# Attention and a squared-ReLU layer on one core: scores in two operations a tile, late loads apart, a new order of all work

## Chip, core and metric

The kernel runs on one core of a Trainium2 chip. Time is device microseconds of a whole execution. A core has five engines that work side by side and wait for each other by semaphores: PE (TensorE, matrix products), DVE (VectorE), ACT (ScalarE), POOL (GpSimd, which here mostly issues transfers) and SP (SyncE, which issues the others). Each runs its own instructions strictly in the order in which they were written.

## What is computed

```python
# q, k, v: 4 batches, 8 heads, 768 positions, 64 wide; local window 96, 8 global keys
scores = q @ k.T / sqrt(64) - slope[h] * dist          # kept where global or local
a = softmax(scores); attn = a @ v                       # -> x: 3072 tokens, 512 wide
h = x @ w_in                                            # 512 -> 2048
out = (max(h, 0) ** 2) @ w_out                          # 2048 -> 512, float32
```

## The kernel before

**Tiles.** The 3072 tokens are 24 tiles `j` of 128 (six to a batch), and two tiles are one block `blk` of the second layer, so there are 12 blocks. A tile needs the keys of itself and of the tile before it, but the first of a batch (0, 6, 12, 18) only its own; the eight global keys and values are copied into each tile's key and value buffers (`gk`, `gv`).

**A tile's steps**, with the names that the order list uses. `tr.0.j` and `tr.1.j` transpose q and k on PE (tiles 0 to 7; later tiles are transposed by a transfer, `T.j`, that SP issues), and `T.0.j`, `T.1.j` copy them out of PSUM. `sc.j` are the scores: 16 small matmuls (8 for the first tile of a batch) of contract dimension 64, line 599, into four PSUM banks (two). For tiles 0 to 2 `bias.j` first writes the mask and slope into those banks by matmuls (line 579). `exp.j.odd.g` is the exponential of one bank on ACT, `mul.j.g` multiplies two of them by the masks on DVE, `pv.j.hf` is the product with v for four heads (line 748), `norm.j.hf` the division on DVE. `trx.j` (PE, tiles 0 to 7) or a transfer `xT.j` transposes the result for the second layer.

**The second layer.** Blocks 0 and 1 use plain products `s1.blk.s` (line 1061) with `relu` and `sq` behind them, later blocks a seven-product scheme: `h.blk.g.p1` to `p7` (line 950) with copies `u` and additions `c` between them and squares `q`; then `s2` (lines 1212 and 1339) with the sums `sum`, copies `part` and results `o`, and the store `st`.

**Loads.** q and k of tile 0 come by SP in float32 (`plain`, line 319). All else comes through POOL's queue with a cast to bfloat16: `ld.k.1`, `ld.win.6.0`, `ld.v.0` and so on for the tiles up to 5 and the weights (line 307), and `load.j` for tiles 6 to 23, one operation that issues v, q and k of the tile one behind another (line 310):

```python
def emit_load(e, j=j):
    load_v(j)
    load_part(0, j)
    load_part(1, j)
```

**Order.** Nothing is scheduled at run time. The string `ORDER` lists all operations by name; the program emits them in that order, each on the engine named behind `@` (A is ACT, V is DVE, P is POOL; without it the first that the operation allows), with the PSUM banks named behind the colon. An engine's order is thus the order of its names in the list. Eight matmuls on zeros (line 372) run before the list, and eight more (`warm`, line 532) stand in it.

Of the kernel before, what the change touches and what calls it, by code (L numbers as in the profile page):

```python
# [62 lines left out]
T.1.4@V xT.1@V pv.2.1:0 ld.k.5 ld.win.2.0 exp.3.1.1 gk.3@A ld.win.2.1 norm.2.0 s1.0.3:2 mul.3.0 s1.0.6:4 ld.win.4.0
tr.0.4:7 ld.q.5 ld.v.4 norm.2.1 mul.3.1 relu.0.6@A s1.0.3#2 gv.2@P pv.3.0:3 norm.3.0 trx.2:5 T.0.4@A pv.3.1:6
ld.win.1.0 norm.3.1 ld.win.0.1 xT.2@A sc.4.0:1047 exp.4.1.1 exp.4.1.0 tr.1.5:3 T.1.5@A s1.0.2:5 trx.3:6 xT.3@V
ld.win.0.0 ld.win.5.0 s1.0.2#2 s1.0.2#3 s1.0.2#4 relu.0.3@V exp.4.0.1 ld.v.5 gv.3@P exp.4.0.0 gk.4@V sq.0.6@V
relu.0.2@A s1.1.3:7 ld.win.7.0 relu.1.3@A load.6 s1.1.6:0 mul.4.1 tr.0.5:6 mul.4.0 sq.0.3@V s1.1.2:3 T.0.5@A ld.wout.3
pv.4.0:2 ld.wout.1 sq.0.2@V sc.5.0:4157 ld.wout.0 s1.0.4:6 relu.1.2@A exp.5.1.1 s1.0.1:3 sq.1.3@A exp.5.0.0 relu.0.4@V
s1.1.4:7 ld.wout.2 norm.4.0 pv.4.1:4 gv.4@P norm.4.1 sq.0.4@A load.7 exp.5.1.0 sq.1.2@A relu.1.4@A s1.0.0:6 gate.9
ld.wout.4 mul.5.0 s1.0.0#2 sq.1.4@A s1.0.0#3 s1.1.5:2 trx.4:1 exp.5.0.1 relu.1.6@V s1.1.1:4 ld.wout.5 s1.0.1#2  # L70
relu.1.1@A E0.1 mul.5.1 relu.1.5@A pv.5.0:7 s1.1.7:0 s1.1.0:5 sq.1.1@V norm.5.0 ld.wout.6 E0.0 sq.1.5@V tr.1.6:4
sq.1.6@A pv.5.1:2 relu.1.7@A tr.0.6:7 s1.0.0#4 norm.5.1 xT.4@A sq.1.7@A h.2.0.p2:0 ld.wout.7 T.1.6@V h.2.1.p2:1
trx.5:2 xT.5@V relu.1.0@A sq.1.0@A gate.14 h.2.0.p1:5 xs.2.0 s1.0.5:4 sum.1.2 s1.0.7:2 relu.0.1@A xs.2.1 gate.10
sum.1.0 sum.1.1 relu.0.0@A T.0.6@A sc.6.0:36 wsum.0.0 sum.1.3 sq.0.0@A sq.0.1@A s2.0.0.0:7 relu.0.7@A s2.0.1.0 load.9
exp.6.0.0 xs.2.2 s2.0.2.0 exp.6.1.0 s2.0.3.0 s2.0.0.1:2 s2.0.1.1 wsum.2.0 relu.0.5@A sq.0.7@A s2.0.2.1 load.8 mul.6.0
wsum.1.0 s2.0.3.1 tr.0.7:3 tr.1.7:6 gate.15 isum.0.0 h.2.1.p1:4 T.0.7@A s2.0.4.0 isum.0.1 s2.1.p1.0:3 isum.3.1 T.1.7@A
sq.0.5@A pv.6.0:6 isum.1.1 s2.0.4.1 s2.0.5.1 u.2.0.1@A c.2.0.c11 s2.0.5.0 gate.11 u.2.1.1@A h.2.1.p6 q.2.0.c11@A
isum.1.0 T.8 s2.0.6.1 u.2.1.2@A s2.0.6.0 isum.3.0 pv.6.1:0 h.2.0.p6 wsum.2.1 wsum.0.1 s2.1.p1.1 s2.0.7.1 c.2.1.c11
norm.6.0 gate.13 o.0.1@V st.0.1 s2.0.7.0 h.2.1.p7 part.1.p1@A s2.1.p6.0 u.2.0.2@A o.0.0@A u.2.1.3@A h.2.0.p7 h.2.1.p4
T.9 norm.6.1 wsum.3.0 u.2.0.3@A sc.7.0:1762 c.2.1.c21@A wsum.1.1 h.2.1.p5:0 c.2.1.c22 q.2.1.c11@A s2.1.p2.0:4  # L80
exp.7.1.0 exp.7.0.0 isum.2.1 load.10 h.2.0.p4 exp.7.0.1 mul.7.0 exp.7.1.1 s2.1.p2.1 isum.2.0 s2.2.p1.0:7 q.2.1.c21@A
mul.7.1 h.2.0.p5:1 s2.1.p6.1 part.1.p6@A trx.6:6 gate.12 c.2.0.c21@A load.12 pv.7.0:2 xT.6@A c.2.0.c22 q.2.1.c22@A
q.2.0.c22@A s2.2.p1.1 h.2.1.p3 s2.1.p7.0 wsum.3.1 o.1.p2 norm.7.0 h.2.0.p3 pv.7.1:5 s2.1.p7.1 q.2.0.c21@A st.0.0
c.2.1.c12 s2.1.p5.0 s2.1.p5.1 part.1.p7@A q.2.1.c12@A s2.1.p4.0 T.10 s2.1.p4.1 c.2.0.c12 gk.7@V q.2.0.c12@A o.1.p5
o.1.p4@A sc.8.0:6201 st.1.1 part.2.p1@A s2.1.p3.0 norm.7.1 sum.2.0 sum.2.1 s2.1.p3.1 trx.7:5 xT.7@V o.1.p3 h.3.0.p1:3
exp.8.1.0 gk.8@V h.3.1.p1:2 exp.8.0.0 exp.8.1.1 exp.8.0.1 h.3.0.p2:6 xs.3.0 u.3.1.1@A sc.9.0:1540 s2.2.p6.0 mul.8.0
xs.3.1 mul.8.1 u.3.0.1@A h.3.0.p6 exp.9.0.1 exp.9.1.1 gv.7@V h.3.1.p2:4 c.3.0.c11 h.3.1.p6 c.3.1.c11 exp.9.0.0
pv.8.0:0 s2.2.p6.1 pv.8.1:6 load.11 norm.8.0 u.3.1.2@A s2.2.p2.0:1 sum.2.2 gv.8@P q.3.1.c11@A norm.8.1 xT.8 h.3.1.p7
h.3.0.p5:4 u.3.0.2@A h.3.0.p7 s2.2.p2.1 exp.9.1.0 st.1.0 part.2.p6@A xs.3.2 u.3.1.3@A q.3.0.c11@A h.3.1.p5:0 s2.2.p7.0
u.3.0.3@A mul.9.1 mul.9.0 s2.2.p7.1 c.3.1.c22 T.12 c.3.0.c22 pv.9.0:6 h.3.1.p3 o.2.p2 h.3.0.p4 c.3.1.c12 load.15  # L90
norm.9.0 q.3.1.c22@A h.3.0.p3 s2.3.p1.0:5 s2.3.p1.1 c.3.0.c12 q.3.0.c22@A pv.9.1:0 c.3.0.c21@A part.2.p7@A norm.9.1
q.3.1.c12@A h.3.1.p4 q.3.0.c12@A h.4.0.p1:3 c.3.1.c21@A s2.2.p5.0 part.3.p1@A gk.9@V sc.10.0:6402 s2.2.p5.1
q.3.0.c21@A sum.3.0 sum.3.1 s2.2.p4.0 s2.2.p4.1 exp.10.1.0 sum.2.3 exp.10.0.0 exp.10.0.1 h.4.0.p2:4 T.11 u.4.0.1@A
exp.10.1.1 gk.10@V gv.9@A s2.3.p6.0 o.2.p5 mul.10.0 c.4.0.c11 xT.9 h.4.1.p1:6 o.2.p4@A mul.10.1 s2.2.p3.0 s2.2.p3.1
q.3.1.c21@A s2.3.p2.0:0 sum.3.2 u.4.1.1@A pv.10.0:2 pv.10.1:4 s2.3.p6.1 xs.4.0 gate.17 o.2.p3 part.3.p6@A xs.4.1
s2.3.p2.1 norm.10.0 h.4.0.p6 h.4.1.p6 q.4.0.c11@A gv.10@A norm.10.1 u.4.0.2@A load.13 s2.3.p7.0 sc.11.0:7124 u.4.1.2@A
sum.3.3 h.4.0.p7 h.4.1.p7 xs.4.2 exp.11.1.0 o.3.p2 exp.11.0.0 u.4.0.3@V s2.3.p7.1 sc.12.0:17 exp.11.1.1 exp.11.0.1
gate.16 xT.10 h.4.0.p4 c.4.0.c21@A mul.11.0 st.2.0 mul.11.1 h.4.1.p2:4 c.4.1.c11 exp.12.1.0 s2.3.p5.0 pv.11.0:2
pv.11.1:3 s2.3.p5.1 norm.11.0 part.3.p7@A h.4.0.p5:7 q.4.1.c11@A u.4.1.3@A norm.11.1 h.4.1.p5:4 q.4.0.c21@A gate.20
s2.3.p4.0 c.4.0.c22 load.14 s2.3.p4.1 h.4.0.p3 T.13 gate.18 load.16 c.4.1.c22 exp.12.0.0 h.4.1.p4 q.4.1.c22@A h.4.1.p3  # L100
xT.11 s2.4.p2.0:2 h.5.0.p1:3 q.4.0.c22@A o.3.p5 mul.12.0 c.4.0.c12 o.3.p4@A c.4.1.c21@A u.5.0.1@A c.4.1.c12 T.15
s2.3.p3.0 q.4.0.c12@A s2.3.p3.1 q.4.1.c12@V q.4.1.c21@A h.5.0.p2:1 o.3.p3 sc.13.0:5764 st.3.1 st.2.1 h.5.1.p1:0
# [1329 lines left out]
```

## Time and profile before

| | |
|---|---|
| runs, us | 198.84, 198.79, 200.68; median 198.84 |
| span of the profiled execution, us | 197.6, so that 1.2 us of the median lie around it |
| PE / DVE / ACT / POOL busy, us | 191.9 / 173.2 / 163.0 / 80.4 |
| matmuls on PE | 2776 |
| chain that ended last, by engine | PE 95%, DVE 2% |

The span runs from the first to the last instruction. A group's row gives its busy time, the mean time of one instruction, and the idle time ahead of it with what ended that. The profile lists no own time for the profiled execution, so sums below are made on the span, and the 1.2 us are added.

### The profile page before, as it was taken

How to read it: one execution, taken by the hardware profiler on the slowest of the kernel's cores; microseconds unless marked ns; L12 is line 12 of the kernel's file. 1: busy time of each engine (PE TensorE's matmuls, PEld its weight loads, DVE VectorE, ACT ScalarE, POOL GpSimd, SP SyncE). 2: the span in 40 equal slices, each digit the busy share in tenths (PEclk: the TensorE clock that was granted, in tenths of full speed). 3: DMA queues.
4: the chain of work that ended last, by engine and by line, in shares of the span. 5: the costliest groups of instructions: out<-in, count | busy, mean ns of one | idle time of the engine just before them, and what ended most of it. 6: DMA issues, size and time to landing. Idle time of an engine off the chain costs nothing.

```text
span 197.6 us, 6777 instructions
## 1 busy us (share of the span) xinstructions
PE 191.9 (97%) x2776; PEld 169.6 (86%) x2776; DVE 173.2 (88%) x423; ACT 163.0 (82%) x335; POOL 80.4 (41%) x101
## 2 busy tenths in 40 slices
PE   7989999999999999999999999999999999999993
PEld 3578999866989999899989999989899989999992
DVE  8159869999999999799999999999899999989872
ACT  6379989966999898999789998998989879774750
POOL 8999988586045309603192903080410001000000
PEclk9999999999999999999999999999999999999999
DMA  6999999999999999999999999999695711114023
GB/s 127 153 158 171 181 181 185 182 202 159 139 209 191 75 200 88 145 174 210 151 129 203 114 124 194 160 121 92 136 81 116 154 55 56 27 30 163 0 106 106
DMA packets 111857, 26.91 MB, mean 136 GB/s; under 512 B 103379, under 2 KB 109011, under 8 KB 111827
## 3 DMA queue, kind: packets, MB, share of 16 engines
q0 software_dynamic: 80256, 13.37, 91.8%
q1 hardware_dynamic: 31570, 13.11, 32.5%
q8 instruction: 21, 0.34, 0.6%
q14 instruction: 10, 0.07, 0.1%
HBM read 27.26 MB, written 6.29 MB: 170 GB/s over the span
## 4 chain that ended last, share of the span: by engine, by line
PE 95%; DVE 2%; issue 1%; ACT 0%; DVEq 0%
PE bank L1212 35%; PE bank L950 32%; PE bank L1061 7%; PE bank L599 6%; PE bank L748 5%; PE bank L1339 4%; PE bank L372 2%; PE bank L506 2%; PE bank L532 1%; DVE qkT L433 1%; PE bank L816 1%; PE bank L579 0%; ACT qkT L429 0%; DVE o L1287 0%; DVE v L433 0%
## 5 line engine op out<-in xcount | busy, mean ns | idle before, releaser
L1015 ACT ACTIVATE hs<-hr 128x512 bf16<-128x512 f32 x72 | 44.8, 641 | 5.1 <-DVE hr L995 4.7
L665 ACT ACTIVATE esc<-bank 128x512 bf16<-128x512 f32 x78 | 42.9, 614 | 1.3 <-PE bank L599 1.0
L1212 PE MATMUL bank<-wsum,hsum 128*128 128x256 bf16 x264 | 36.2, 273 | 0.0
L1212 PEld LDWEIGHTS <-hsum 128*128 128x128 bf16 x360 | 32.1, 98 | 4.1 <-issue 0.5
L995 DVE CUSTOM_DVE_ANT_0 hr<-bank,early 128x512 f32<-128x512 f32 x45 | 30.4, 685 | 2.5 <-PE bank L950 1.5
L950 PEld LDWEIGHTS <-win 128*128 128x128 bf16 x480 | 29.7, 98 | 1.0
L950 PEld LDWEIGHTS <-qk_first 128*128 128x128 bf16 x480 | 29.7, 98 | 1.0
L429 ACT COPY early<-bank 128x512 f32<-128x512 f32 x42 | 24.5, 591 | 3.6 <-PE bank L950 3.3
L690 DVE TENSOR_TENSOR at<-esc,E 128x1024 bf16<-128x1024 bf16 x39 | 26.7, 696 | 0.1
L1212 PEld LDWEIGHTS <-hs 128*128 128x128 bf16 x264 | 24.0, 98 | 2.6
L310 POOL DMA_DIRECT2D qk<-in_q_dram x18 | 16.0, 890 | 21.9 <-DMA qkT<-qk 20.6
L1212 PE MATMUL bank<-wout,hs 128*128 128x256 bf16 x176 | 24.9, 273 | 0.0
L310 POOL DMA_DIRECT2D v<-in_v_dram x18 | 16.0, 888 | 18.3 <-DVE v L480 14.9
L950 PE MATMUL bank<-xT,win 128*128 128x128 bf16 x320 | 23.4, 219 | 0.0
L431 POOL COPY v<-v 8x520 bf16<-8x520 bf16 x8 | 5.7, 718 | 43.3 <-PE bank L748 43.3
L950 PE MATMUL bank<-xs,qk_first 128*128 128x128 bf16 x320 | 22.8, 219 | 0.0
L779 DVE TENSOR_TENSOR x<-bank,rs 128x256 bf16<-128x256 f32 x48 | 20.4, 425 | 1.7
L865 ACT ACTIVATE hr<-bank 128x512 f32<-128x512 f32 x33 | 19.4, 598 | 1.3 <-PE bank L950 0.4
L748 PE MATMUL bank<-v,at 128*128 128x65 bf16 x352 | 17.8, 193 | 0.0
L1287 DVE TENSOR_TENSOR o<-bank,part 128x256 f32<-128x256 f32 (+2 forms) x34 | 13.8, 410 | 3.3 <-PE bank L1212 3.2
L429 ACT COPY part<-bank 128x256 f32<-128x256 f32 x29 | 10.9, 375 | 7.1 <-PE bank L1212 6.9
L310 POOL DMA_DIRECT2D qk<-in_k_dram x18 | 16.1, 897 | 0.9 <-DMA win<-in_moe_w_in_dram 0.5
(92 smaller groups left out, 367.0 us busy)
## 6 DMA issues: line engine op xcount, KB each, us to landing
out_dram<-o SPq DMA_DIRECT2D x22, 256.0 KB, 2.5
v<-in_v_dram POOLq DMA_DIRECT2D x24, 128.0 KB, 5.6
qk<-in_q_dram POOLq DMA_DIRECT2D x18, 128.0 KB, 5.0
qk<-in_k_dram POOLq DMA_DIRECT2D x18, 128.0 KB, 5.8
wout<-in_moe_w_out_dram POOLq DMA_DIRECT2D x8, 256.0 KB, 8.5
win<-in_moe_w_in_dram POOLq DMA_DIRECT2D x6, 256.0 KB, 6.9
...
```

What stands on the lines that cost most here:

```text
L310: nc.gpsimd.dma_start(out=dst, in_=src)
L429: nc.scalar.copy(dst, src)
L665: nc.scalar.activation(out=tiles[tag, j, g][:, odd], in_=tiles.pop(("sc", j, odd, g)).rearrange("p a c -> p (a c)"), func=Act.Exp, scale=s ...
L690: nc.vector.tensor_mul(at, tiles.pop(("esc", j, g)), bias)
L748: nc.tensor.matmul(out=po[:, hi, :], lhsT=tiles["at", j, g][:, odd, at * P : (at + 1) * P], rhs=v_sb[kj][:, h, :], start=(i == 0), stop=(i ...
L779: nc.vector.tensor_tensor(out=x[:, 4 * hf : 4 * hf + 4, :], in0=po[:, :, :D], in1=rs.to_broadcast([P, 4, D]), op=Alu.mult,)
L865: nc.scalar.activation(dst, src, Act.Relu)
L950: nc.tensor.matmul(out=tiles["h", blk, g, bank][:, n], lhsT=left_[:, s, k], rhs=right_[:, k], start=opens and n == 0 and k == 0, stop=k == ...
L995: nc.vector._custom_dve(TENSOR_ADD_SAT, out=hr, in0=src, in1=tiles.pop(("u", blk, g, i)), s0=float("inf"), s1=0.0,)
L1015: nc.scalar.activation(hs, hr, Act.Square)
L1061: nc.tensor.matmul(out=hT[:, c, cols], lhsT=w_in_sb[s][:, kt, c * P : (c + 1) * P], rhs=tiles["xT", blk][:, kt, cols], start=(kt == 0), st ...
L1212: nc.tensor.matmul(out=tiles["acc", blk, bank][:, cols], lhsT=left_[:, s], rhs=right_[:, cols], start=first and s == 0, stop=s == NSTEP - ...
```

## The change

Four edits. (1) The scores of a tile that isn't the first of its batch become two operations, `sc.j.0` (heads 0 to 3) and `sc.j.1` (heads 4 to 7), each with two banks; so do the `bias` matmuls of tiles 1 and 2. The matmuls are the same. (2) `load.j` becomes `lv.j`, `lq.j` and `lk.j`, each with a wait of its own and a place of its own. (3) `warm` asks for its bank like other operations. (4) `ORDER` is another list throughout: other places, other banks, and for some copies another engine.

```diff
 ORDER = """
-tr.0.0:0 warm:7 tr.1.0:1 T.1.0@V bias.0.0:23 T.0.0@A sc.0.0 ld.win.3.0 exp.0.0.0 ld.k.1 tr.1.1:4 bias.1.0:5670 T.1.1@V ld.q.1
-tr.0.1:1 ld.v.0 exp.0.1.0 T.0.1@V sc.1.0 exp.1.0.1 pv.0.0:2 ld.q.2 tr.0.2:3 norm.0.0 ld.k.2 T.0.2@V ld.k.3 exp.1.1.1
-pv.0.1:4 tr.1.2:1 bias.2.0:7203 ld.v.1 norm.0.1 exp.1.1.0 ld.q.3 tr.1.3:6 gk.1@A T.1.2@A sc.2.0 exp.1.0.0 T.1.3@V
...
+ld.k.1 ld.win.6.0 ld.q.2 ld.q.1 tr.0.0:0 ld.win.2.1 ones.6 ld.k.2 tr.1.0:1 T.0.0@A ld.k.3 warm:2 T.1.0 E0.0 ld.v.0
+ld.v.1 bias.0.0:23 sc.0.0 ld.q.3 tr.0.2:4 exp.0.0.0 tr.0.1:5 T.0.2 tr.1.1:6 ld.win.2.0 bias.1.0:70 T.0.1 T.1.1@A
+bias.1.1:12 ld.v.2 exp.0.1.0 sc.1.1 sc.1.0 exp.1.0.1 ld.q.4 tr.1.2:4 gk.1 bias.2.0:56 exp.1.0.0 T.1.2 tr.1.3:3 exp.1.1.1
...
-    SETS = {}
+    SETS = {j: [(0,), (1,)] for j in range(NT) if j % TPB}
...
-            def emit_load(e, j=j):
-                load_v(j)
-                load_part(0, j)
-                load_part(1, j)
...
-            ld = plan.op(
-                ("load", j), {"POOLQ": 2.6}, emit_load,
-                deps=qk_users[slot(j)] + v_users[j % NV] + [ones.get(j), gate], key=base, ready=issue[0],
-            )
+            for name, f, users in (
+                ("lv", load_v, v_users[j % NV] + [ones.get(j), gate]),
+                ("lq", lambda j: load_part(0, j), qk_users[slot(j)]),
+                ("lk", lambda j: load_part(1, j), qk_users[slot(j)]),
+            ):
+                ld = plan.op(
+                    (name, j), {"POOLQ": 0.9}, lambda e, j=j, f=f: f(j), deps=users, key=base, ready=issue[0],
+                )
+                land[name[1], j] = plan.op(("data" + name, j), {"DMAQ": 2.7}, None, deps=[ld])
...
-            plan.op(("warm",), {"PE": 0.216 * NKEEP}, emit_warm, key=base)
+            wusers = []
+            wusers.append(plan.op(
+                ("warm",), {"PE": 0.216 * NKEEP}, emit_warm, key=base, takes=(*G, [wusers]),
+            ))
```

Three places show what the list moves. **PE at the start.** `plain` is q of tile 0 (into bank 0) and then k of tile 0 (into bank 1); DMAHW1 is the landing of that k. Before, the transposes of q were followed by the eight `warm` matmuls, of which the first row below is the last, and by these:

```order
L532 MATMUL bank_7_114<-early_103 128x512
L506 MATMUL bank_1_108<-ident32_100,plain_70 128x128 [waits DMAHW1_49]
L506 MATMUL bank_1_108<-ident32_100,plain_70 128x128 x3
L579 LDWEIGHTS early_103 [waits DVE_49]
L579 MATMUL bank_2_109<-pb0_105,early_103 128x128
```

and now, from the transposes of q to the first `warm`:

```order
L502 MATMUL bank_0_107<-ident32_100,plain_70 128x128 [waits DMAHW0_49,DVE_49]
L502 MATMUL bank_0_107<-ident32_100,plain_70 128x128 x3
L502 MATMUL bank_1_108<-ident32_100,plain_70 128x128 [waits DMAHW1_49]
L502 MATMUL bank_1_108<-ident32_100,plain_70 128x128 x3
L528 LDWEIGHTS early_103
L528 MATMUL bank_2_109<-early_103 128x512
```

The eight `warm` matmuls stood ahead of the transposes of k, and stand behind them now.

**POOL's queue at the start.** Before (`qk_first` holds q and k of tiles 1 to 5: k1, q1, then q2, k2 and k3, then q3, k4; v_71, v_72 and v_73 are v of tiles 0, 1 and 2):

```order
L307 DMA win<-in_moe_w_in_dram 128x4x256
L307 DMA qk_first<-in_k_dram 128x8x64
L307 DMA qk_first<-in_q_dram 128x8x64
L307 DMA v_71<-in_v_dram 128x8x64
L307 DMA qk_first<-in_q_dram 128x8x64
L307 DMA qk_first<-in_k_dram 128x8x64 x2
L307 DMA v_72<-in_v_dram 128x8x64
L307 DMA qk_first<-in_q_dram 128x8x64
L307 DMA qk_first<-in_k_dram 128x8x64
L307 DMA v_73<-in_v_dram 128x8x64
```

and now (k1; q2 and q1; k2 and k3; q3):

```order
L305 DMA qk_first<-in_k_dram 128x8x64
L305 DMA win<-in_moe_w_in_dram 128x4x256
L305 DMA qk_first<-in_q_dram 128x8x64 x2
L305 DMA win<-in_moe_w_in_dram 128x4x128
L305 DMA qk_first<-in_k_dram 128x8x64 x2
L305 DMA v_71<-in_v_dram 128x8x64
L305 DMA v_72<-in_v_dram 128x8x64
L305 DMA qk_first<-in_q_dram 128x8x64
L305 DMA win<-in_moe_w_in_dram 128x4x128
L305 DMA v_73<-in_v_dram 128x8x64
```

v of tile 2 was the eleventh transfer of the queue and is the twelfth, with two half pieces of w_in ahead of it beside a whole one.

**PE around tile 2's product with v.** Before, `pv.2.0` followed the scores of tile 3 and the transposes of tile 1's result:

```order
L816 MATMUL bank_7_114<-ident_99,x_319 128x128
L748 LDWEIGHTS at_315
L748 MATMUL bank_5_112<-v_2_73,at_315 128x65 [waits DMASW2_49]
L748 LDWEIGHTS at_315
L748 MATMUL bank_5_112<-v_1_72,at_315 128x65 [waits DVE_49]
```

Now it follows the transposes of q of tile 3 (`qk_first`), and the scores of tile 3 stand behind it:

```order
L502 MATMUL bank_6_113<-ident_99,qk_first_66 128x128
L747 LDWEIGHTS at_305 [waits Activation_49]
L747 MATMUL bank_4_111<-v_2_73,at_305 128x65 [waits DMASW3_49]
L747 LDWEIGHTS at_305
L747 MATMUL bank_4_111<-v_1_72,at_305 128x65 [waits DVE_49]
```

The wait on DMASW is that for v of tile 2. Behind it on PE are now `sc.3.0` and `sc.3.1`, side by side. On PE the two halves of a tile stand side by side in all of the 20 split tiles but tile 2, and twice the scores of two tiles stand together (7 and 6, 18 and 17), so PE comes to scores 23 times where it came 24 times.

More of the change, by code (lines that the diff above doesn't have):

```diff
@@ L63 @@
[L63 to L102, printed above, removed]
@@ new lines @@
+T.1.4 lk.6 s1.0.2#3 relu.0.6 norm.3.0 pv.3.1:0 sc.4.1:71 sq.0.6 sc.4.0:24 ld.win.1.0 norm.3.1 s1.0.0:6 exp.4.0.0
+s1.0.0#2 gate.12 xT.2 ld.v.5 trx.3:0 exp.4.1.1 s1.0.2#4 xT.3 s1.0.0#3 exp.4.1.0 s1.0.0#4 gk.4 lk.7 s1.1.0:2 relu.0.0
+mul.4.0 ld.win.4.0 tr.1.5:5 E0.1 relu.1.0 tr.0.5:1 s1.1.6:0 lq.7 T.0.5@A T.1.5 sq.0.0@V exp.4.0.1 s1.0.3:4 lq.6 sq.1.0
+gv.3 sc.5.1:62 mul.4.1 sc.5.0:51 exp.5.1.1 ld.win.7.0 s1.0.3#2 relu.1.6@V exp.5.0.1 pv.4.0:7 s1.1.3:2 ld.win.5.0 sq.1.6
+norm.4.0 exp.5.1.0 mul.5.1 ld.wout.0 pv.4.1:0 tr.1.6:6 relu.0.2 s1.1.1:7 norm.4.1 ld.wout.2 exp.5.0.0 T.1.6@A gv.4@P
@@ L161 @@
+sum.11.1#2 part.11.p1 sum.11.2 s2.10.p3.1 q.11.0.c21 o.10.p4@V s2.11.p6.0 sum.11.3#2 s2.11.p6.1 o.10.p3 sum.11.3
+s2.11.p2.0:1 st.10.0 part.11.p6 sum.11.2#2 s2.11.p2.1 s2.11.p7.0 o.11.p2 s2.11.p7.1 st.11.0 s2.11.p5.0 part.11.p7@V
+st.10.1 s2.11.p5.1 s2.11.p4.0 s2.11.p4.1 o.11.p4 o.11.p5 st.11.1 s2.11.p3.0 s2.11.p3.1 st.11.1#2 s2.11.p3.0#2
+s2.11.p3.1#2 o.11.p3 st.11.0#2 o.11.p3#2 st.11.0#3
 """
```

151 lines of the change are left out of this document (89 added, 62 removed).

## The prediction, made before the changed kernel ran

> **What bounds the kernel now.** I read the page's shares and its chain first, then the waits of PE by themselves, then PE's start in order of time.
>
> ```profile
> span 197.6 us, 6777 instructions
> ...
> PE 191.9 (97%) x2776; PEld 169.6 (86%) x2776; DVE 173.2 (88%) x423; ACT 163.0 (82%) x335; POOL 80.4 (41%) x101
> ...
> PE 95%; DVE 2%; issue 1%; ACT 0%; DVEq 0%
> ```
>
> The chain that ended last is PE for 95% of the span. A busy PE need not be at its pace, so the next view is the waits of PE alone from 20 to 195 us (total, times, longest), and behind it pieces of the chain in order of time (start, length, line, matmuls).
>
> ```profile
> PE bank L1212 <- DVE o L1287: 0.5, 1, 0.5
> ```
>
> ```profile
> 79.12 0.89 PE bank L950 x16
> ...
> 80.45 0.55 PE bank L599 x16
> 81.00 1.00 PE bank L950 x16
> 82.00 0.44 PE bank L1212 x4
> 82.44 0.33 PE bank L599 x8
> 82.77 1.00 PE bank L950 x16
> ```
>
> In 175 us PE waits once, for 0.5 us, and that is in the tail. Pieces follow each other without a gap, each at a fixed pace: 0.89/16 = 56 ns for a matmul of line 950, 0.44/4 = 110 ns for one of line 1212. So from 20 us on the time is a sum of matmuls, the same 2776 before and after. Only four things can change it: when PE's unbroken run begins, what it costs PE to come to the scores, new waits inside the run, and the tail. A quicker path of scores to exponentials is worth nothing by itself there.
>
> **Term 1, the start.** Pieces of the chain in the first microseconds, and then PE in order of time; in brackets idle time and who ended it.
>
> ```profile
> 4.79 0.85 PE bank L506 x4
> 5.64 2.41 PE bank L532 x8
> 8.05 0.45 PE bank L506 x4
> ...
> 10.00 0.87 PE bank L579 x8
> 10.88 0.24 PE bank L506 x4
> ```
>
> ```profile
> 1.19 3.60 PE L372 MATMUL bank<-early 128*128 128x512 bf16 x8 [1.19 <-DVE early L361]
> ...
> 9.28 0.40 PE L599 MATMUL bank<-qkT 64*128 64x128 bf16 x8 [0.34 <-DVE qkT L433]
> ...
> 11.62 0.23 PE L599 MATMUL bank<-qkT 64*128 64x128 bf16 x2 [0.52 <-DVE qkT L433]
> ...
> 16.65 0.23 PE L599 MATMUL bank<-qkT 64*128 64x128 bf16 x2 [0.29 <-DVE qkT L433]
> ...
> 17.44 0.85 PE L748 MATMUL bank<-v,at 128*128 128x65 bf16 x16
> 18.12 1.49 PE L1061 MATMUL bank<-xT,win 128*128 128x128 bf16 x16
> ```
>
> The run begins at 18.12, with the first product of the second layer. What the new list makes of that point depends on two landings.
>
> *k of tile 0.* `tr.1.0` now stands ahead of `warm`, so PE waits for that k with nothing to do.
>
> ```profile
> 1.25 0.56 SPq L319 DMA_DIRECT2D plain<-in_k_dram  x1
> ```
>
> ```profile
> plain<-in_q_dram SPq DMA_DIRECT2D x1, 256.0 KB, 3.1
> plain<-in_k_dram SPq DMA_DIRECT2D x1, 256.0 KB, 6.0
> ```
>
> It landed at 1.25 + 6.0 = 7.25, which the warm matmuls covered before; q, of the same size, took 3.1, by which k would be there at 4.35. The transposes of q end at 4.79 + 0.85 = 5.64. So the wait is between nothing and 1.6 us. I take 0.5, a landing near 6.1, since the first transfer of POOL's queue beside it is now half as large. Then `tr.1.0` ends near 6.6, `warm` (2.41) near 9.0, `bias.0` (eight matmuls of 128 columns, 56 ns each as on line 950) near 9.4, and `sc.0` starts there instead of at 9.28: the copy behind `tr.1.0`, which cost 0.34 us of waiting, now lies under `warm`.
>
> *v of tile 2.* In the new list `pv.2.0` stands ahead of the scores of tile 3. From `sc.0` to it PE has six groups of transposes at 0.23, the chain's 0.24 or a little under, `bias.1` and `bias.2` at 0.87 each, the scores of tiles 0, 1 and 2 (0.4, 0.6 and, in two pieces, 0.85), and `pv.0`, `pv.1` and `trx.0` (about 0.95; the two products of 17.44 take 0.68 together): 5.9 us, which would put `pv.2.0` near 15.4. But its v comes later.
>
> ```profile
> L307 POOL DMA_DIRECT2D v<-in_v_dram x1: 913/913/913, 4.0 to 4.0; - x1
> DMA to landing us min/median/max: 5.7/5.7/5.7
> L307 POOL DMA_DIRECT2D v<-in_v_dram x1: 972/972/972, 10.0 to 10.0; - x1
> DMA to landing us min/median/max: 5.6/5.6/5.6
> ```
>
> These are v of tiles 0 and 2, the fourth and the eleventh transfer: landed at 9.7 and 15.6, seven transfers of 128 KB in 5.9 us, 0.85 us each. The queue is the pace here. In the new list one transfer of 128 KB more stands ahead, so v of tile 2 lands at 15.6 + 0.85 = 16.45, a microsecond after PE could use it. `pv.2.0` therefore waits, and a delay of up to 1 us at k of tile 0 costs nothing. Behind it come `pv.2.0` (0.24), `sc.3` (0.65), `trx.1` (0.24) and `pv.2.1` (0.24), and the run begins at 17.8. Before it began at 18.12, but with the transposes `tr.1.4` (0.22) already done, so the point to compare is 17.9. The term is -0.1. Its ends: without any wait for v the run begins 1.0 earlier; with the waits of before on top of the new chain (0.34, 0.52 and 0.29 above, and as much again between pieces of the chain that aren't PE's), of which the wait for v hides 1.0, about 1.3 later.
>
> **Term 2, coming to the scores.** From the pieces above, 16 score matmuls take 0.55 and eight take 0.33, so 27 ns each and 0.11 fixed; the 16 matmuls of line 950 behind them take 1.00 where they take 0.89 elsewhere. Coming to the scores and leaving them costs 0.2 us. If each half stood by itself, 20 more visits would cost 4 us. They don't: the new order has 23 visits for 24 (apart in tile 2 alone, four tiles joined in pairs), so the term is -0.2; the ends are -0.4 and 0, since a joined pair may have to wait for a bank between its halves.
>
> The Trainium skill, TensorEngine Tiling (Array Packing), section Key Properties, says that a change of tiling mode drains TensorE. The scores are the only matmuls of 64 rows here (64*128 in the rows), so the extra on both sides agrees with it; read as a rule for this change, it would make the split a loss of 4 us wherever the halves part.
>
> **Term 3, new waits in the run.** Between 20 and 190 us, from a window of that stretch:
>
> ```profile
> 20.00:190.00 170.00, 170.00 (x2529) 153.39 (x2526) 158.50 (x367) 148.70 (x304) 61.23 (x74) 1.00 1.22 134
> ```
>
> ```profile
> L433 DVE COPY part<-bank 128x256 f32<-128x256 f32 x4 | 1.6, 412 | 0.0
> L433 DVE COPY early<-bank 128x512 f32<-128x512 f32 x3 | 2.1, 692 | 1.7 <-ACT esc L665 1.6
> ```
>
> The columns after the window's length are PE, PEld, DVE, ACT and POOL. DVE idles 11.5 of 170 us. The new list gives DVE six more `part` copies (0.41 each), two `u` (0.69), two `q` (0.69), and smaller copies to a balance of about 5.8 us, and takes 7 to 8 from ACT. DVE's idle time halves, and each late addition `c` holds a bank that PE needs. Against that, the list leaves more room elsewhere: counted in PE's own pieces between the two names in the list, the transposing transfers of tiles 8 to 23 stand at least 7 us ahead of their scores (2.2 at the least before), and the transfers `xT` 6 us ahead of `xs` (0.9). Bounds: nothing, as now, to 2 us (a wait of 0.5, like the one seen, in four of the ten late blocks). I take 0.2, near the lower end, since the row for 175 us of the present run has no wait outside the tail.
>
> The loads apart cost nothing by themselves: the same 54 transfers in the same queue, and their issue lies beside PE's run.
>
> ```profile
> L310 POOL DMA_DIRECT2D qk<-in_q_dram x18 | 16.0, 890 | 21.9 <-DMA qkT<-qk 20.6
> ```
>
> At 0.89 us each they leave POOL, 41% busy in all, with 21.9 us in which it waited for a buffer ahead of q alone. Queued behind a waiting load are only other loads and the copies `gv`; without the cover, a load that came later than its transposes would cost PE the difference, which the distances above bound.
>
> **Term 4, the tail.**
>
> ```profile
> 194.16 0.36 DVE L1287 TENSOR_TENSOR o<-bank,part 128x192 f32<-128x192 f32 x1 [0.84 <-PE bank L1212]
> 194.57 0.28 PE L1212 MATMUL bank<-wout,hsum 128*128 128x64 bf16 x4 [0.45 <-DVE o L1287]
> 194.88 0.22 DVE L1287 TENSOR_TENSOR o<-bank,part 128x64 f32<-128x64 f32 x1 [0.37 <-PE bank L1212]
> ```
>
> The last four matmuls (`s2.11.p3.1#2`) now stand ahead of the addition `o.11.p3`. PE's wait of 0.45 goes, but the addition of 192 columns then waits for those matmuls, 0.2 later, and the two additions follow each other: the last ends near 195.0 for 195.1, and the store of the 192 columns is issued 0.2 later. The term is 0, between -0.1 and +0.2.
>
> **The sum.** -0.1 - 0.2 + 0.2 + 0 = -0.1, on the span 197.5, and with the 1.2 us around it 198.7 against a median of 198.84. A run of this kernel tells 1% from no change, 2 us, and this is far inside that.
>
> **Rivals.**
> *The start is slower (loss).* The first matmuls of 512 columns take 3.60/8 = 0.45 us, those of `warm` 2.41/8 = 0.30 between their starts, so PE comes to its full pace inside `warm`. If k of tile 0 lands at 7.25 as now, PE idles 1.6 us and the slow pace may last through all that follows: `tr.1.0` ends at 8.1, eight `warm` at 0.45 end at 11.7, `bias.0` at 0.9 ends at 12.6, and `sc.0` starts 3.3 us later than before. The wait for v hides 1.1 of it, so 198.7 + 2.1 = 200.8. It decides if the pace is not full by the time `warm` starts. For it: 7.25 is what was measured; against it: before the pause PE has been busy for 4.4 us without a break. The skill's TensorE: Matmul & The Clock Gate, Part 1, has the array at half clock until a window of about 3.4 us is busy, and back there after an idle one; by that a pause of 1.6 us may cost one window more, and no trace here shows such a pause.
> *DVE becomes the bound (loss).* Where DVE's work between two blocks exceeds PE's, every block waits; a late addition in each of ten blocks at 0.3 us gives 201.7, in half of them 200.2. For it: the halved idle time; against it: windows of before in which DVE is 98% busy (19.65 of 20 us from 40 to 60) and PE still doesn't wait.
>
> ```profile
> 40.00:60.00 20.00, 20.00 (x244) 15.62 (x243) 19.65 (x45) 16.33 (x34) 10.10 (x13) 1.00 1.64 177
> ```
>
> *The run begins a microsecond earlier (gain).* If POOL's queue gets going sooner with a small first transfer, v of tile 2 is there at 15.4: 197.7. Against it: seven transfers in 5.9 us is a steady rate.
> *The split does nothing.* That is within the forecast: with the halves side by side, PE's sum is untouched.
>
> **How the numbers follow.** Forecast 0.64, between 198.0 and 199.6 (terms 1 to 3 at half of their bounds). Earlier start 0.12 (197.5 to 198.0). Slower start 0.11 (199.6 to 201). DVE 0.13 (199.6 to 201.7). The range 197.6 to 200.6 leaves out about 2 in 10 of the rivals' ends and no more. Faster by over 1% (under 196.85) needs more than all the waits of the start: 0.04. Slower by over 1% (over 200.83) is the upper part of both losses: 0.12. The rest, 0.84, is within 1%.
>
> **What would show it.** Right: PE's scores come in 23 visits; `pv.2.0` starts near 16.5 behind a wait for the transfer of v; the first matmul of line 1060 (1061 before) is near 17.8; PE shows under 0.5 us of waits from 20 us on; the wait of 0.45 in the tail is gone. Wrong: waits of PE on DVE by the dozen after 20 us; `sc.0` past 11 us with matmuls of `warm` at 0.45 us; k of tile 0 landing later than 7.25.

## The result, and the profile after

The changed kernel is slower: 201.15 us median (200.08 to 205.34, 13 runs) against 199.07 for the kernel before on the same chip, ratio 1.0087, 95% interval 1.0057 to 1.0116, about 1.7 us. The forecast was 198.7, the range ended at 200.6. Disturbed runs, over 1.5% longer than the fastest of the same kernel, are left out of the ratios here and below. Each ratio is to runs of the kernel before that were made in the same session, so a difference between two ratios carries the uncertainty of both.

The profiled execution of the changed kernel took 201.33 us with a span of 199.6, 2.0 us more than the span before. First the page, then PE's waits from 20 to 195 us (total, times, longest), then the window of 20 to 190 us (busy time of PE, PEld, DVE, ACT, POOL), which stand against the same three views of before:

```profile
span 199.6 us, 6775 instructions
...
PE 192.5 (96%) x2776; PEld 170.6 (85%) x2776; DVE 178.0 (89%) x434; ACT 157.3 (79%) x321; POOL 82.3 (41%) x104
...
PE 74%; POOL 10%; DMA 7%; ACT 4%; issue 1%; DVE 1%; DVEq 0%; ACTq 0%; POOLq 0%
```

```profile
PE bank L949 <- ACT early L427: 0.5, 2, 0.3
PE bank L949 <- DVE xs L921: 0.4, 1, 0.4
PE bank L747 <- POOL v L429: 0.2, 1, 0.2
```

```profile
20.00:190.00 170.00, 168.93 (x2502) 152.50 (x2500) 160.32 (x369) 141.86 (x288) 63.08 (x78) 1.00 1.27 134
```

PE's share of the chain fell from 95% to 74%: the unbroken run is broken. The fall is no measure of the time lost, though. At 29.8 PE pauses 0.41 us for a copy on POOL, and from there the chain goes back through POOL's queue to the start, past stretches in which PE was busy too; a second piece is one transposing transfer (start, length, line):

```profile
1.34 1.01 POOL qk_first L305
...
19.94 7.11 DMA win<-in_moe_w_in_dram
...
29.12 0.67 POOL v L429
29.83 0.61 PE bank L747 x15
...
110.13 7.68 DMA xT<-x
```

Three releasers stand in the waits where there was one, and the one named most is ACT, which has 6.8 us *less* work in this window than before (141.86 against 148.70); DVE, with 1.8 us more, is named once.

The waits of this view sum to 1.1 us, but a matmul's row runs on for 0.16 us past the place where the next one starts (eight of line 949 show 0.61 us and follow each other at 0.45), so shorter pauses do not show there. Taken from start to start of the matmuls, PE's pauses between 20 and 190 us sum to 2.6 us. There are three kinds of them, each with the rows around it in order of time:

```profile
105.29 1.50 PE L949 MATMUL bank<-xs,qk_first 128*128 128x128 bf16 x24
...
106.35 0.39 ACT L427 COPY part<-bank 128x256 f32<-128x256 f32 x1
...
106.80 0.60 PE L1211 MATMUL bank<-wsum,hs 128*128 128x256 bf16 x4
```

```profile
28.41 0.71 POOL L305 DMA_DIRECT2D wout<-in_moe_w_out_dram  x1
...
29.12 0.66 POOL L429 COPY v<-v 8x520 bf16<-8x520 bf16 x1
...
29.83 0.61 PE L747 MATMUL bank<-v,at 128*128 128x65 bf16 x15 [0.24 <-POOL v L429]
...
117.90 0.43 DVE L921 TENSOR_TENSOR xs<-xT 128x512 bf16<-128x512 bf16 x1 [0.91 <-DMA xT<-x]
...
118.71 0.62 PE L949 MATMUL bank<-xs,qk_first 128*128 128x128 bf16 x8 [0.37 <-DVE xs L921]
...
124.19 0.61 PE L949 MATMUL bank<-xs,qk_first 128*128 128x128 bf16 x8 [0.29 <-ACT early L427]
```

*A copy out of a bank is late.* The 24 matmuls at 105.29 take 24 x 0.056 = 1.34 us, so the next could start near 106.63; the next product needs the bank that ACT's copy `part.4.p7` empties at 106.74. That copy stood behind an exponential that nobody waited for. Such pauses are at 106.6 (0.16), 123.6, 136.4 (0.15), 149.7 (0.33) and 174.2 (0.15).
*A copy waits behind transfers.* On POOL, `gv.4` stands behind the issue of the first two transfers of w_out, and POOL had idled 0.93 ahead of these for the landing of a piece of w_in; PE pauses for 0.41.
*A transposing transfer lands late.* `xT.15` lands at 117.8, DVE has idled 0.91 for it, PE pauses 0.53. DVE's next operations and ACT's behind them are late too, so that at 123.6 the pause is 0.45.

The chain of 149.7 shows the first kind best (start, length, line):

```profile
146.56 0.37 ACT part L427
146.93 0.12 ACT qkT L427
147.05 0.53 ACT hs L1014
147.58 0.52 ACT kl L427
...
148.12 0.22 ACT kl L427
148.33 0.54 ACT hs L1014
...
149.39 0.59 ACT early L427
149.98 0.04 issue
150.02 0.61 PE bank L949 x8
```

The chain leaves PE for ACT's queue: 0.74 us of it is `kl.22`, a copy for scores that come 6 us later (those of tile 23). It has no hurry, but `u.9.0.1` (the last ACT row), which PE needs, stands behind it.

Start and tail, in PE's rows, the landing of k of tile 0, and the last rows of DVE and SP:

```profile
4.58 1.68 PE L502 MATMUL bank<-ident,plain 128*128 128x128 f32 x8
6.09 1.89 PE L528 MATMUL bank<-early 128*128 128x512 bf16 x8
...
16.21 0.40 PE L747 MATMUL bank<-v,at 128*128 128x65 bf16 x8 [0.71 <-DMA v<-in_v_dram]
...
17.57 0.61 PE L1060 MATMUL bank<-xT,win 128*128 128x128 bf16 x8
```

```profile
plain<-in_k_dram SPq DMA_DIRECT2D x1, 256.0 KB, 3.9
```

```profile
194.82 2.58 SPq L1308 DMA_DIRECT2D out_dram<-o  x4
...
195.04 1.06 PE L1211 MATMUL bank<-wout,hsum 128*128 128x192 bf16 x16
...
196.21 0.49 DVE L1286 TENSOR_TENSOR o<-bank,part 128x192 f32<-128x192 f32 x2 [1.41 <-PE bank L1211]
```

So the 2.0 us of the span: the start gives 0.3, the scores inside the run 0.4 (18 visits for 20 from 20 us on; 23 for 24 in all), the pauses cost 2.6, the tail 0.1.

### The profile page after: what moved, and what is told of

It is laid out like the page before. It is cut to its first block, busy times and chain, and to the rows that moved or that the text cites. A ratio compares the mean times of both kernels' runs of the same rounds, so it can differ in the third digit from the quotient of the medians.

```text
span 199.6 us, 6775 instructions
## 1 busy us (share of the span) xinstructions
PE 192.5 (96%) x2776; PEld 170.6 (85%) x2776; DVE 178.0 (89%) x434; ACT 157.3 (79%) x321; POOL 82.3 (41%) x104
## 4 chain that ended last, share of the span: by engine, by line
PE 74%; POOL 10%; DMA 7%; ACT 4%; issue 1%; DVE 1%; DVEq 0%; ACTq 0%; POOLq 0%
PE bank L1211 30%; PE bank L949 29%; POOL qk_first L305 4%; PE bank L598 4%; PE bank L747 4%; DMA xT<-x 4%; DMA win<-in_moe_w_in_dram 4%; PE bank L1338 3%; PE bank L1060 3%; POOL win L305 2%; POOL v L305 2%; ACT hs L1014 1%; ACT early L427 1%; ACT kl L427 1%; POOL wout L305 1%
## 5 line engine op out<-in xcount | busy, mean ns | idle before, releaser
L1014 ACT ACTIVATE hs<-hr 128x512 bf16<-128x512 f32 x70 | 43.5, 641 | 6.3 <-DVE hr L994 6.2
L664 ACT ACTIVATE esc<-bank 128x512 bf16<-128x512 f32 x78 | 44.0, 612 | 5.3 <-DVE at L689 2.9
L1211 PEld LDWEIGHTS <-hsum 128*128 128x128 bf16 x360 | 32.6, 98 | 3.7
L1211 PE MATMUL bank<-wsum,hsum 128*128 128x256 bf16 x264 | 35.2, 273 | 0.0
L1211 PE MATMUL bank<-wout,hs 128*128 128x256 bf16 x176 | 24.4, 272 | 0.0
L949 PE MATMUL bank<-xs,qk_first 128*128 128x128 bf16 x320 | 23.6, 219 | 0.8 <-ACT early L427 0.5
L429 POOL COPY v<-v 8x520 bf16<-8x520 bf16 x11 | 7.4, 674 | 35.3 <-PE bank L747 35.3
L747 PE MATMUL bank<-v,at 128*128 128x65 bf16 x352 | 18.4, 193 | 1.2 <-DMA v<-in_v_dram 0.9
L747 PEld LDWEIGHTS <-at 128*128 128x128 bf16 x352 | 15.9, 98 | 2.8 <-issue 1.2
```

Of the source, the lines that this page charges most:

```text
L664: nc.scalar.activation(out=tiles[tag, j, g][:, odd], in_=tiles.pop(("sc", j, odd, g)).rearrange("p a c -> p (a c)"), func=Act.Exp, scale=s ...
L747: nc.tensor.matmul(out=po[:, hi, :], lhsT=tiles["at", j, g][:, odd, at * P : (at + 1) * P], rhs=v_sb[kj][:, h, :], start=(i == 0), stop=(i ...
L949: nc.tensor.matmul(out=tiles["h", blk, g, bank][:, n], lhsT=left_[:, s, k], rhs=right_[:, k], start=opens and n == 0 and k == 0, stop=k == ...
L1014: nc.scalar.activation(hs, hr, Act.Square)
L1211: nc.tensor.matmul(out=tiles["acc", blk, bank][:, cols], lhsT=left_[:, s], rhs=right_[:, cols], start=first and s == 0, stop=s == NSTEP - ...
```

## The experiments

Two theories stood against each other. **A**: every pause has its own late instruction, and goes when that one is earlier. **B**: DVE and ACT carry too much in this list, so that a pause taken away comes back elsewhere. The names in the diffs are those of the order list, and most lines are pieces of longer lines; numbers in the expectations are absolute times of the changed kernel's first session.

**One copy earlier on POOL (e_gv).**

```diff
-ld.wout.2 exp.5.0.0 T.1.6@A gv.4@P
+exp.5.0.0 T.1.6@A gv.4@P ld.wout.2
```

> The changed kernel with one move in GpSimd's queue: the copy gv.4 stands ahead of the second transfer of w_out instead of behind it. Theory A (each wait of TensorE after 20 us has its own late instruction, and goes when that instruction is earlier): the pause of 0.41 us between the first and the second matmul of pv.5 at 29.4 us disappears, nothing takes its place, time 0.2 to 0.4 us below the changed kernel's 201.15, so about 200.8. Theory B (VectorE and ScalarE have too much to do, and TensorE waits for them sooner or later): the pause goes, but TensorE waits as long somewhere in the next 20 us, and the time stays at 201.1.

Ratio 1.0080 (1.0057 to 1.0104). In its trace the pause at 29.4 is gone. 0.4 us is less than this comparison resolves, so the time alone decides nothing. Nor does the trace: among the runs below that leave this copy where it was, e_xt has the pause (0.37), while in e_ld, e_v2 and e_act POOL issued w_out earlier, the copy was in time, and 0.25 to 0.5 us stand one matmul earlier (in e_ld for DVE's `at`). This pause comes and goes from execution to execution.

**One transposing transfer behind another (e_xt).**

```diff
-T.19 exp.16.1.1
+exp.16.1.1
...
-o.4.p4@V xT.15
+o.4.p4@V xT.15 T.19
```

> The changed kernel with one move in SyncE's queue: the transposing transfer T.19 stands behind xT.15 instead of ahead of it. Theory A1 (transposing transfers are worked off one after the other, so xT.15, issued at 110.1 and landed at 117.8, waited for T.19, landed at 113.9): xT.15 lands near 114, the wait of 0.42 us of TensorE for xs at 118.6 goes and with it the two that follow from it (0.09 at 119.7 and 0.45 at 123.6); about 0.9 us less than the changed kernel, near 200.2. Theory A2 (xT.15 is slow because loads move beside it, whatever stands ahead): it still takes over 7 us, and the time stays at 201.1. Theory B (VectorE and ScalarE are overloaded): the wait for xs goes, that at 123.6 stays, 0.4 us less at most.

Ratio 1.0058 (1.0031 to 1.0085). `xT.15` took 5.8 us where it took 7.7, and the wait for `xs` is gone; of the pause at 123 a part of 0.16 stayed. But in the run before this one, where T.19 stood ahead as always, the transfer happened to take 6.4 and the wait was gone too. This pause comes and goes as well, and A1 is not shown.

**Two loads behind two others (e_ld).**

```diff
-lk.21 s2.4.p3.0
+s2.4.p3.0
...
-lq.21 norm.15.0
+norm.15.0
...
-T.20 s2.5.p5.0 lq.22
+T.20 s2.5.p5.0 lq.22 lk.21 lq.21
```

> The changed kernel with the loads lk.21 and lq.21 moved in GpSimd's queue from ahead of gv.15 to behind lq.22, so that between 107 and 114 us one load moves instead of three. Theory A2 (loads beside them make the transposing transfers slow): T.19 and xT.15, which took 7.3 and 7.7 us from issue to landing, take 3 to 5, xT.15 lands before 115, the wait for xs at 118.6 and its two successors go, about 0.9 us less, near 200.2. Theory A1 (only the queue of transposing transfers counts): T.19 lands near 113.9 and xT.15 near 117.8 as before, time 201.1.

Ratio 1.0077 (1.0046 to 1.0108). `xT.15` took 4.7, as A2 has it, but T.19 still took 7.1. Half a confirmation, and no time.

**v of tile 2 one transfer earlier (e_v2).**

```diff
-tr.1.1:6 ld.win.2.0 bias.1.0:70 T.0.1 T.1.1@A
-bias.1.1:12 ld.v.2 exp.0.1.0
+tr.1.1:6 ld.v.2 bias.1.0:70 T.0.1 T.1.1@A
+bias.1.1:12 ld.win.2.0 exp.0.1.0
```

> The changed kernel with v of tile 2 one place earlier in GpSimd's queue, ahead of the half piece of w_in that stood before it. If the queue's pace of about 0.8 us a transfer sets the start (term 1 of the prediction): v lands at 15.4 instead of 16.16, the wait ahead of pv.2.0 falls from 0.71 to about 0, the unbroken run begins 0.6 to 0.75 us earlier (near 16.9 instead of 17.57), and the time falls by as much, to about 200.5. If something else is late behind it (the scores' exponentials, or the half piece of w_in, now landing near 16.0), 0.2 us or less.

Ratio 1.0070 (1.0034 to 1.0106). The run began at 17.50 instead of 17.57. PE's rows of this run say why:

```profile
6.20 0.66 PE L502 MATMUL bank<-ident,plain 128*128 128x128 f32 x4 [0.56 <-DMA plain<-in_k_dram]
6.69 1.89 PE L528 MATMUL bank<-early 128*128 128x512 bf16 x8
...
16.13 0.37 PE L747 MATMUL bank<-v,at 128*128 128x65 bf16 x7 [0.29 <-DVE v L431]
```

v was no longer late, but in this execution PE waited 0.56 for k of tile 0, and behind the wait for v stood a copy of the global rows of v on DVE. What was late was replaced by what was late next. This profile also has two longer pauses that the other profiles of this list lack: 0.85 near 32, for the landing of a load of q, and 0.90 near 79, behind the transposing transfer of tile 9.

**Five copies earlier (e_act).**

```diff
-exp.16.0.0 h.6.0.p5:7 gate.17 xs.6.2 part.4.p7
+part.4.p7 exp.16.0.0 h.6.0.p5:7 gate.17 xs.6.2
...
-q.6.1.c21 s2.5.p3.0 c.7.1.c22 T.22 pv.17.0:5 u.7.0.1
+s2.5.p3.0 c.7.1.c22 T.22 pv.17.0:5 u.7.0.1 q.6.1.c21
...
-s2.6.p7.1 q.8.0.c11 xs.8.2 h.8.0.p6 part.6.p7
+s2.6.p7.1 part.6.p7 q.8.0.c11 xs.8.2 h.8.0.p6
...
-kl.22@A xs.9.2
+xs.9.2
...
-h.9.1.p1:5 u.9.0.1
+h.9.1.p1:5 u.9.0.1 kl.22@A
...
-part.9.p6@V
+part.9.p6@A
```

> The changed kernel with five moves that make a copy out of a bank earlier than work that nobody waits for: kl.22 behind u.9.0.1, q.6.1.c21 behind u.7.0.1, part.4.p7 ahead of exp.16.0.0, part.6.p7 ahead of q.8.0.c11, and part.9.p6 on ScalarE instead of VectorE. They answer to the five pauses of TensorE that every profile of this list so far shows near 106.6, 123, 136, 149 and 174 us (0.16, 0.16, 0.15, 0.33 and 0.15 us). Theory A (each pause has its own late copy): the five go, about 0.95 us in sum, and the time is 0.8 to 0.95 us below the changed kernel, a ratio to the kernel before near 1.004. Theory B (VectorE and ScalarE carry too much in this list, so pauses come back elsewhere): the ratio stays near 1.008.

Ratio 1.0031 (1.0008 to 1.0054), 0.56% or 1.1 us below the changed kernel, with an uncertainty of 0.37%; theory A has 0.95 us. Its window of 20 to 190 us:

```profile
20.00:190.00 170.00, 169.90 (x2520) 154.04 (x2518) 161.82 (x374) 143.55 (x292) 62.78 (x78) 1.00 1.36 134
```

PE's idle time in the window falls from 1.07 to 0.10 us, and from start to start its pauses fall from 2.6 to 0.5. Not all of that is the edit: the pauses behind `gv.4` and `xT.15`, which it doesn't touch, were absent in this execution as in others. The five are the edit: they stand in the profiles of the changed kernel, e_gv, e_xt, e_ld, e_v2 and e_lessv, at nearly the same sizes (only that at 123 grows when `xT.15` is late), and in none of the four whose list moves these copies (this one, e_all2, e_tail2, e_late). DVE is busier than before (161.82 for 160.32) though it gave a copy away, since more of the work falls into the window. No work was taken out: four copies changed places with work that nobody waited for, and one went from DVE to ACT. For these five, theory B falls.

**All of it together (e_all2).** The edits of e_act, e_gv, e_xt and e_v2.

> All moves together: the five copies, gv.4 earlier, T.19 behind xT.15, v of tile 2 one transfer earlier. Theory A: TensorE has under 0.5 us of pauses after 20 us, and the time is that of the changed kernel less 0.95 (copies), 0.4 (gv.4), what the wait for xs cost on average (0 to 0.9), and 0.3 to 0.7 (start): 2 us less than the changed kernel and the same as the kernel before or a little better, ratio 0.997 to 1.001. Theory B: pauses move, ratio 1.005 or more.

Ratio 0.9992 (0.9964 to 1.0021): the time of the kernel before. It scatters more, though: over all twelve runs the median is 200.00, and single runs reach 204.03, where those of before have 199.75 and 200.36. In its trace the view of waits has none of PE between 20 and 195 us. PE's last matmul ends at 194.0 for 194.85 before, of which 0.6, from start to start, is the wait of the tail that is gone; the last landing, at 196.45 for 196.58, shows that the drain takes this back.

**The halves apart (e_apart).** In ten tiles, as for tile 14:

```diff
-sc.14.0:76 o.3.p4@V sc.14.1:41 u.5.0.3 sum.4.0 pv.13.0:2
+sc.14.0:76 o.3.p4@V u.5.0.3 sum.4.0 pv.13.0:2 sc.14.1:41
```

> The changed kernel with the second half of the scores of ten tiles (8, 10, 11, 13, 14, 15, 16, 19, 21, 22) put behind the next product on TensorE, so that TensorE comes to scores 33 times instead of 23. By term 2 of the prediction (0.2 us for coming to scores and leaving them) the time is 2.0 us above the changed kernel, ratio near 1.019. If the extra belongs to each score matmul and not to the visit, the time stays, ratio 1.009.

Ratio 1.0167 (1.0154 to 1.0181): 0.80%, 1.6 us more than the changed kernel for ten visits. Pieces of its chain with tile 10, whose halves stand around a product:

```profile
63.43 0.33 PE bank L598 x8
63.76 0.54 PE bank L1211 x4
64.30 0.35 PE bank L598 x8
```

Two visits of eight cost 0.33 and 0.35 where one of 16 cost 0.55, and the product between them 0.54 where it costs 0.44: 0.23 us for the visit, against the 0.2 of term 2. The time, 0.16 a visit, is the same within the comparison's 0.07.

**The split taken back (e_join, e_alljoin).** Eighteen tiles have one operation of 16 matmuls again, at the place of the second half; once in the changed kernel, once in e_all2.

```diff
-SETS = {j: [(0,), (1,)] for j in range(NT) if j % TPB}
+SETS = {j: [(0,), (1,)] for j in (1, 2)}
...
-sc.14.0:76 o.3.p4@V sc.14.1:41
+o.3.p4@V sc.14.0:7641
```

> The changed kernel with the split taken back for 18 of the 20 tiles (3 to 23 but for the first of each batch): the two halves, which stand side by side, are one operation again, at the place of the second half. All other places are those of the changed list. If the split itself matters (the first exponential 0.3 us earlier, banks taken one pair at a time), this is slower than the changed kernel by what ScalarE then lacks: 0.3 us or more, ratio 1.010 or more. If the split does nothing with the halves side by side, the same within 0.2 us, ratio 1.0087. If taking four banks at one point saves a wait, up to 0.3 us faster.

> The version with all moves (ratio 0.9992) with the split taken back for 18 tiles, as in the earlier run in which the split was taken back in the changed kernel (ratio 1.0118, with 2.4 us in one wait for a late transposing transfer in its profile). If the split does nothing with halves side by side, and the earlier excess was that transfer: ratio 0.998 to 1.001, score visits still 23, no new wait of TensorE over 0.2 us. If the earlier exponentials and the banks taken in pairs are worth something: ratio 1.002 or more, with waits of TensorE for ScalarE's copies or exponentials behind the scores.

Ratios 1.0118 (1.0079 to 1.0157) and 1.0031 (1.0004 to 1.0059): 0.31% and 0.39% slower than with the split, about as much as the uncertainties of these differences (0.5 and 0.4%). DVE's row in e_join that precedes its longest pause of PE (2.4 us):

```profile
79.39 0.43 DVE L921 TENSOR_TENSOR xs<-xT 128x512 bf16<-128x512 bf16 x1 [3.07 <-DMA xT<-x]
```

The transposing transfer of tile 9 landed at 79.4, in the changed kernel at 75.7. Whether the split or the transfer was the cause was left to the last pair.

**Less data beside the transposing transfers (e_lessv).** The loads of v of tiles 10 to 23 bring 8 of 128 rows; the rest of the rows is left as it was.

```diff
-swdge(("v", j), v_sb[j][:, :, :D], src_rows(v, j).rearrange("h p d -> p h d"), 0.87)
+swdge(("v", j), v_sb[j][: 8 if j >= NV else P, :, :D],
+      src_rows(v, j)[:, : 8 if j >= NV else P].rearrange("h p d -> p h d"), 0.87)
```

> The changed kernel with the loads of v of tiles 10 to 23 cut to 8 of the 128 rows (those rows of v stay as an earlier tile left them): the same transfers in the same queue and places, a sixteenth of the data in 14 of the 54 loads of q, k and v. Theory A2 (the transposing transfers are slow because loads move beside them): between 40 and 125 us the transposing transfers of x, 6.7 us from issue to landing in the changed kernel and 4.3 in the one before, fall below 5.5, VectorE never idles ahead of xs, and the time falls by what such waits cost on average, 0.3 to 0.9 us: ratio 1.003 to 1.006. If what makes them slow is other than data moving beside them (their own order in SyncE's queue, or their number), 6 to 7 us as before and ratio 1.0087.

Ratio 1.0045 (1.0026 to 1.0065), 0.42% or 0.8 us below the changed kernel with an uncertainty of 0.35%, so hardly beyond it. All twelve runs lie between 199.82 and 200.74, where the changed kernel's compared runs lie between 200.08 and 203.06. The transposing transfers of x between 40 and 125 us, from issue to landing, before, in the changed kernel and here:

```profile
DMA to landing us min/median/max: 2.5/4.3/5.1
```

```profile
DMA to landing us min/median/max: 4.7/6.7/7.9
```

```profile
DMA to landing us min/median/max: 2.4/4.5/5.8
```

So data that moves beside these transfers makes them slower in this list: e_gv, e_xt, e_ld, e_v2, e_act, e_all2 and e_tail2, with all loads whole, have medians of 6.1 to 6.7. That this is also the difference to the kernel before is not shown. In this stretch POOL's queue moves 6.57 MB where it moved 6.22, little more, and e_apart, with 6.60 MB, has a median of 4.9; where the loads fall beside the transfers must count too. The Trainium skill, DMA: Bandwidth & Descriptors, section Queues, rings and completion order, says that each DMA engine takes turns between the queues that have work for it, a packet at a time; that agrees with a transposing transfer that takes 6.7 us beside full loads and 4.5 beside short ones.

**The loads together again (e_merge).** As shown for tile 6, so for tiles 6 to 23, with lv beside them in nine tiles:

```diff
-T.1.4 lk.6 s1.0.2#3
+T.1.4 s1.0.2#3
...
-s1.0.3:4 lq.6 sq.1.0
+s1.0.3:4 lq.6 lk.6 sq.1.0
```

> The changed kernel with its loads together again: lq and lk of each late tile stand side by side at the place of the later one, in nine tiles lv with them; nothing else moves. If loading apart is what let loads run far ahead and beside the transposing transfers (A2), those take less than 5.5 us between 40 and 125 us, and the time is 0.3 to 0.9 us under the changed kernel, ratio 1.003 to 1.006. If the order of all work does it and the loads apart do nothing: transposing transfers near 6 us, ratio 1.0087. If loads apart help (a transfer that now comes later than its use), TensorE waits for a transposed tile: ratio over 1.011.

Ratio 1.0683 (1.0651 to 1.0715). Two waits of PE make most of it:

```profile
PE bank L502 <- DMA qk<-in_k_dram: 4.4, 1, 4.4
PE bank L949 <- DVE xs L921: 4.2, 2, 3.8
```

k of tile 6 now comes 4.4 us after PE could transpose it, and at 144.7 `xs` waits for a transposing transfer that landed 7.4 us after its issue. The places of this list lean on loads that go singly, as soon as a buffer is free; putting them together at the later place is not the change undone, and it says nothing on what loads apart cost by themselves.

**The tail of before (e_tail2).** On e_all2:

```diff
-s2.11.p3.1#2 o.11.p3 st.11.0#2
+o.11.p3 s2.11.p3.1#2 st.11.0#2
```

> The version with all moves (ratio 0.9992) with the end in the order of the kernel before: the addition o.11.p3 ahead of the last four matmuls. By term 4 the two orders are worth the same: TensorE waits 0.45 us again, and from its end to the last landing it is 1.7 us instead of 2.4; the sum 0.1 to 0.2 us less, ratio 0.998 to 0.999. If the two stores issued close behind each other at the end are the price (0.43 us on SyncE between them), up to 0.3 us less.

Ratio 1.0016 (0.9982 to 1.0050): no difference that can be told. In the traces the last landing is at 196.07 for 196.45, of which 0.2 is the earlier start of this execution.

**Loads of v later (e_late), and the split taken back there (e_latejoin).** On e_all2, five loads of v move behind loads of q and k that wait for a buffer:

```diff
-gk.10 lv.13 s2.2.p6.0
+gk.10 s2.2.p6.0
...
-o.2.p3 lv.16 h.4.0.p7
+o.2.p3 lv.13 h.4.0.p7
...
-exp.15.1.0 lk.20 s2.4.p2.1
+exp.15.1.0 lk.20 lv.16 s2.4.p2.1
...
-s2.5.p5.0 lq.22
+s2.5.p5.0 lq.22 lv.19 lv.20
```

> The version with all moves (ratio 0.9992, single runs 198.9 to 204.0) with five loads of v that stood 20 to 50 us ahead of their use put later in GpSimd's queue (v of tile 13 from 70 to 81 us, 18 from 76 to 96, 16 from 81 to 99, 19 and 20 from 102 to 119): the same data, out of the stretches in which the transposing transfers of x for tiles 9, 10, 14 and 15 move. Theory A2 (loads beside them make those transfers late): the transposing transfer of tile 9 takes under 5.5 us (5.5 to 8.3 in the runs so far) and VectorE doesn't idle ahead of xs; single runs scatter by under 1.5 us, ratio 0.995 to 0.998. If the loads only shift the crowd to other transfers: ratio 0.999 or above, with as much scatter.

> The same with the split taken back for 18 tiles. If the 0.3 to 0.4% that this cost twice came from the late transposing transfer of tile 9 (2.5 and 3.5 us of wait in the two profiles): the same ratio as the version beside it within 0.1%. If the exponentials that start later and the four banks taken at one point cost it: again 0.3% above that version, with waits of TensorE spread over the late tiles.

Ratios 1.0033 (0.9993 to 1.0072) and 1.0101 (1.0054 to 1.0148). The first is a miss: DVE never idled ahead of `xs` in the profile, but the runs scatter as widely as those of e_all2 (198.95 to 201.61), and the time is no better. I read it as a crowd that was moved and not thinned, which no run tests. The second is 0.68% slower than the first, and its profile has the same late transfer again:

```profile
78.50 0.43 DVE L921 TENSOR_TENSOR xs<-xT 128x512 bf16<-128x512 bf16 x1 [2.72 <-DMA xT<-x]
```

Three times out of three, the list without the split was slower, by 0.31, 0.39 and 0.68% (the three together: 0.4% with an uncertainty of 0.3%). So the split itself is a gain in this list, of about 0.4%. Where it comes from is only partly seen. In all three traces PE pauses behind the first matmul of a tile's scores at three places, 0.16 us near 20, 0.28 near 100 and 0.13 near 154, where the lists with the split have no pause. That is 0.57 us; I take it to be a bank that PE would need later with the split, which is not shown. And the transfer of tile 9 lands at 78.5 to 79.5, where it landed at 75.2 to 77.8 in the lists with the split and full loads (but at 80.2 in e_merge). Why it does stays open. It is no matter of the split alone, since e_v2 has a milder case, and the profile of e_alljoin is that of its longest execution (204.26 us).

No version beats the kernel before clearly; e_all2 equals it.

## Why the prediction failed, by its own steps

**What bounds the kernel.** Right as a reading of before: PE's run had no pause, and the ten added visits (1.6 us) show that PE's own time is the kernel's time.

**Term 1, the start (-0.1).** Right, at -0.3. The run began at 17.57 for a forecast of 17.8, `pv.2.0` waited for v as foreseen, and v landed at 16.16 for 16.45. The wait for k of tile 0 was a matter of chance, as its bounds said: 3.9 us to land here, so no pause at all, 0.56 and 0.88 us of pause in e_v2 and e_merge. The rival of the slow pace finds nothing for it in these two: after each of the two pauses the eight `warm` matmuls took 1.89 us, 0.22 each between their starts. A pause of 1.6 us, as it assumed, came in no profile. The Trainium skill, TensorE: Matmul & The Clock Gate, Part 1, has the clock fall after an idle window of about 3.4 us; the traces agree in that a pause of 0.88 us doesn't do it.

**Term 2, the visits (-0.2).** Right: 23 visits, and 0.23 us for one by e_apart's pieces, 0.16 by its time.

**Term 3, new waits (+0.2, bounds 0 to 2).** This is the step that failed: 2.6 us in the profile, beyond its upper end, and 1.6 to 1.7 in those of e_gv, e_xt and e_ld. Of this 0.95 us, the five late copies, stands in all of them, and e_all2 gives back 0.95% of the time (1.9 us, the start's edit among them). The reason that I gave for 0.2, that the run of before had no wait outside the tail, speaks of the old list alone, where other instructions stood ahead of the copies. The step failed in three places.
- I looked for the late engine by its load. The list gives DVE more work and ACT less, so I priced late additions on DVE and gave ACT, relieved of 7 us, no term. ACT's copies were the late ones in four of the five places, and DVE's in one. ACT, 83% busy in this window, was late for an instruction that stood behind three others.
- I counted room between two names in PE's time (`xT` 6 us ahead of `xs`, against 0.9 before) and took the transfer's own time as given. It took 4.3 us before and 6.7 after, up to 7.9. For `xT.15` the slower transfer used up the wider room in this profile; in those of e_gv, e_v2 and e_act, which leave that transfer and its neighbours where they were, it did not, so this part of the 2.6 is chance.
- The sentence on the queue behind a waiting load was too light: "the copies `gv`" stood there, and one of them held PE for 0.41, in this profile and in that of e_xt.

**Term 4, the tail (0, bounds -0.1 to +0.2).** Right: +0.1. PE's wait of 0.45 went. From PE's end to the last landing it is 2.4 us (196.10 to 198.54) where it was 1.7 (194.85 to 196.58), since both additions and both last stores now follow PE's end.

**The split does nothing.** Wrong in sign of a small thing: with the halves side by side it is worth about 0.4%, and without it the new list would be slower still.

**The base.** Of the later runs the span is known, and most of both kernels lie 1.7 to 1.8 us over it. The 1.2 that I added to the span of before was the difference to a median of other executions; with 1.75, the same sum gives 199.25.

**The rival that came nearest** was the one in which an engine beside PE is late at many blocks (200.2 to 201.7), with nearly the right time and the wrong engine, and five steady pauses for its ten. It had 0.13; what spoke against it, a busy window without pauses, was the argument that doesn't hold: four of the five steady pauses went when copies changed places and no work was taken away.
